# A fused sliding-window attention and expert-attention kernel: outputs of the last batch in two parts, one transfer for the last 64 rows, a new order list

## The chip, the cores and the metric

The kernel runs on one NeuronCore of one Trainium2 chip. The metric is the device time of one launch in microseconds, as the median of several runs. Inputs and outputs lie in device memory (DRAM); the core computes from its on-chip memory (SBUF) and accumulates matmuls in eight PSUM banks of 128 x 512 floats. Five engines work beside each other, each with its own instruction queue, in program order: TensorE (PE, matmuls; PEld are its weight loads), VectorE (DVE), ScalarE (ACT), GpSimd (POOL), and SyncE (SP), which here only issues transfers. Engines wait for each other through semaphores.

## What is computed

Eight batches of 576 positions. First an attention over a window of 32 positions on either side, with 8 heads of 64; its output, heads side by side, is `x` of the second part: four experts, each a causal attention over all 576 positions with a head size of 64 and an output projection to 512, of which each position adds up its best two by a gate.

```python
scores = q @ k.T / 8;  mask = abs(pos[:, None] - pos[None, :]) <= 32
attn = softmax(where(mask, scores, -1e9));  x = heads_side_by_side(attn @ v)      # [8, 576, 512]

logits = x @ w_gate;  topk = best 2 of 4;  w = softmax(logits of those 2)
for e in range(4):
    a = softmax(causal((x @ wq[e]) @ (x @ wk[e]).T / 8))
    ye = a @ (x @ wv[e]) @ wo[e]
    out += where(e in topk, w[e], 0) * ye                                          # [8, 576, 512] float32
```

## The kernel before

The whole program is written out by hand as a list of steps, `ORDER` (lines 27 to 89). The loop at the end (line 607) takes one step after the other and calls the function of that name, which emits its instructions. As every engine runs its own instructions in program order, the list sets, for each engine, what stands before what; between engines only data and buffers make anyone wait. A step reads `name` + digits + optional `:engine` + optional `@banks`: `sc601@62` is the score matmuls of batch 6, head group 0, second half of the columns, into banks 6, 7 and 2, 3; `ye52:v@7` copies an output of batch 5 from bank 7 on VectorE. The letters behind the colon are v, g and a for VectorE, GpSimd and ScalarE; a load with `e` is issued by SP, with `f` by ScalarE's queue.

The steps of one batch, in the order in which data goes:

- `lq`, `lk`, `lv`: loads of q, k and v. A load waits for the last matmul that stands ahead of it in the list. `tq`, `tk` transpose q and k on VectorE, two instructions each. `vc` makes a shifted copy of v.
- `sc`, `ex`, `mk`: window scores (80 matmuls for one half of one head group), their exponential on ScalarE, their mask as a product on GpSimd or VectorE.
- `av`, `un`: probabilities times v, and the division by the sum (VectorE). `xt`, `xf`, `xb`: transposition of the result on TensorE, its copy out of PSUM, its copy to bf16. A `zz` is four matmuls of zeros.
- `ga`, `gt`, `ge`, `gm`, `gu`: the gate: matmul, transposition and maximum, exponential, choice of two, weights. `gu` is four small VectorE instructions.
- `pp`, `pe`: q and k of two experts (pair `j`), and their copy out of PSUM; `pv`, `ve`: the same for v.
- `ps`, `xe`, `se`: causal scores, their exponential (ScalarE), their mask (GpSimd).
- `po`, `oe`: for pair `j` of experts, probabilities times v in five tiles of 128 positions and two experts, 30 matmuls; then on VectorE a reciprocal of the sums, its product with the gate's weight, and the product with the result, into `OE`.
- `dt`: a transposing transfer of `OE` into `OTT`, issued by SP. For batch 7 the turn is made on TensorE in its place (`pt`, five transposes into one bank, and `ot`, the copy into `OTT`).
- `py`, `ye`, `st`: the output projection from `OTT`, its copy into a buffer `Y`, the store. `w` is 0 or 1 for 256 positions each and 2 for the last 64. In batch 7, `w` 0 and 1 are split into single tiles of 128 (`py701` is batch 7, `w` 0, second tile).

There are three buffers `Y`, chosen by `YSB[(3 * b + w) % 3]`, so by `w` alone: a copy `ye` of batch b waits until the store of the same `w` of batch b - 1 has landed. For `w` = 2 the 64 positions lie as two halves of the 512 columns on 128 partitions, and line 597 stores each half by a transfer of its own.

Of the kernel before, what the change touches and what calls it, by code (L numbers as in the profile page):

```python
# [9 lines left out]
BF16 = mybir.dt.bfloat16  # L10
# [9 lines left out]
S = 576  # L20
# [7 lines left out]
    s_zero s_ones lk000:e lq000:e lv03 lk012:e tk000:e lq011:f zz1@0 zz0@0 lq012:e lk011:e s_ident s_mask lq100:e  # L28
    tq000:e sc000@02 lk100:e s_warm ex0001@2 tq011:e ex0000@0 sc001@46 ex0010@4 lv01 lv02 zz4@0 tk012:e tq012:e
    tk011:e sc010@02 mk0001:g mk0000:v ex0100@0 tq100:e lv00 tk100:e ex0101@2 zz2@4 lk110:e sc011@40 ex0011@6 zz3@2  # L30
    ex0110@4 mk0011:g vc00:a lv04 s_pads lq110:e lw00 sc101@26 vc01:a mk0101:v mk0100:v lw11 ex0111@0 av01@4 un01@4
    mk0110:g mk0010:g mk0111:g av00@0 un00@0 av04@4 lw2 xt00@0 un04@4 xf00:a@0 av03@4 ex1010@2 ex1011@6 tk110:e lw01
    av02@0 lq200:e un03@4 sc100@26 lk200:e xt02@4 ex1001@6 xf02:a@4 un02@0 xt01@0 xb02:a tq110:e mk1011:g sc110@64
    ex1000@2 xb00:g cw11:g xf01:v@0 lw10 tq200:e cw01:g mk1000:g cw2:g sc111@20 ex1101@4 xb01:a cw10:g lv13 lv11
    pp011@4 ex1100@6 lwg cw00:a tk200:e pp010@6 lv12 lv10 ex1110@2 pp000@2 pe011:a@4 pe000:v@2 pp001@4 ex1111@0
    sc201@02 lq210:e pe001:v@4 pe010:a@6 ps002@6 mk1010:v ga0@4 mk1111:v mk1110:v mk1100:v lv14 mk1101:g mk1001:g
    vc10:g ex2010@0 vc11:g lk210:e gt0@4 ps001@0 xe002@6 se002 ex2011@2 xe001@0 pv00@6 sc200@20 lq300:e tq210:e
    ve00:a@6 ex2000@2 av12@6 un12@6 ex2001@0 ps011@2 xe011@2 lq310:e ge0@4 av13@0 un13@0 ps000@2 pv01@5 xe000@2 av10@6
    tk210:e ps03@0 lv21 un10@6 xt11@2 ve01:a@5 xe03@0 av11@0 xf11:a@2 lk300:e un11@0 lv22 av14@5 ps010@2 un14@5 gm0@4
    xt10@6 xf10:v@6 xe010@2 xt12@5 xf12:a@5 sc211@02 lv20 lv24 tq300:e lv23 xb12:a ex2110@0 ga1@5 gt1@5 gu0@4 sc210@60  # L40
    ex2111@2 xb11:a mk2010:g mk2000:g se010 mk2011:g xb10:g lq400:e mk2001:g pp110@2 ex2100@6 ex2101@0 pp101@6 ge1@5
    tk300:e pp111@0 pe110:a@2 pe101:a@6 vc20:a mk2111:g mk2101:g se011 lw3 lk310:e pe111:v@0 gm1@5 gu1@5 tq310:e
    mk2100:g vc21:g pp100@2 pe100:a@2 pv11@4 sc300@60 mk2110:g ex3000@6 ex3001@0 pv10@2 ve10:a@2 av21@6 lq410:e av23@0
    un21@6 av22@2 un23@0 ps101@6 un22@2 lv32 ps100@0 av24@5 cw3:g se000 mk3000:g se001 xe100@0 xe101@6 se03 un24@5
    xt21@2 lv31 xt22@5 lk400:e xf22:v@5 xf21:a@2 ve11:v@4 xb22:g ps012@0 av20@6 sc301@24 un20@6 xt20@6 xe012@0
    ex3011@4 lv33 tk310:e ex3010@2 mk3001:g xb21:g se012 xf20:a@6 po00@0 lq500:e ps13@4 ps112@2 po01@6 xe112@2 oe00@0
    xe13@4 ps102@0 xe102@0 sc311@24 oe01@6 mk3011:g mk3010:g ex3111@4 lk500:e xb20:g sc310@60 pp201@4 ex3110@2 lv30
    lk410:e ex3100@6 ex3101@0 ps111@2 ps110@6 pp200@0 pe201:a@4 tk400:e xe111@2 lv34 pp211@4 tq400:e pp210@2 xe110@6
    lv42 pe210:a@2 pe200:v@0 pe211:v@4 tq410:e pv20@6 ve20:a@6 sc400@02 mk3101:g mk3111:g mk3100:g vc31:g se101
    mk3110:g dt00 se100 vc30:g tk410:e dt01 ex4000@0 ex4001@2 lv40 sc401@46 ps202@0 ga2@2 ex4011@6 mk4011:g se110 se13  # L50
    mk4001:g se102 lv43 pv21@3 av33@6 lq600:e xe202@0 av30@0 ve21:a@3 ex4010@4 gt2@2 py02@3 ge2@2 ye02:a@3 lk600:e
    av32@4 gm2@2 un33@6 un30@0 av34@3 py01@6 lv41 ye01:a@6 gu2@2 un32@4 un34@3 po10@0 xt32@2 lv50 xf32:a@2 av31@4
    ps23@6 xe23@6 oe10@0 ps211@2 un31@4 xe211@2 xt31@0 ps210@6 mk4000:g xe210@6 sc411@42 xf31:v@0 lv51 lq510:e xt30@0
    ex4110@4 ex4111@2 tk500:e tq500:e xf30:a@0 sc410@64 ex4101@4 py00@2 ye00:v@2 ex4100@6 se112 xb32:g mk4010:g se111
    xb31:g ps201@0 vc41:g ps200@4 xb30:g se202 vc40:g pp301@6 xe201@0 xe200@4 pp311@0 lk510:e pe301:v@6 sc501@24
    pe311:a@0 sc500@60 ex5010@2 tq510:e lv44 pp300@2 ex5011@4 lv53 ex5000@6 pp310@4 po11@6 ex5001@0 pe300:a@2 tk600:e
    pe310:a@4 oe11@6 ps300@0 ps301@2 mk4101:g mk4110:g mk4111:g av43@4 se200 mk4100:g lk610:e pv31@6 xe300@0 av40@0
    xe301@2 av41@2 un43@4 un40@0 ve31:a@6 lv54 av42@4 un41@2 ps212@6 dt10 ps302@0 xe212@6 ga3@2 xe302@0 av44@3 un42@4
    ps33@4 xe33@4 tq600:e dt11 un44@3 st00 xt41@6 xf41:a@6 lv61 lv52 xt40@0 gt3@2 ge3@2 gm3@2 xt42@3 xf40:a@0 xf42:a@3
    sc600@46 ex6001@6 ex6000@4 mk5000:g lq610:e tk510:e mk5010:g se201 se300 se210 se302 xb41:g se212 se23 se211  # L60
    xb42:a pv30@0 gu3@2 lv63 ve30:v@0 xb40:a sc510@64 mk5011:g ex5100@6 lv64 lq710:e pp401@2 pe401:a@2 pp411@0
    pe411:a@0 po20@6 oe20@6 st02 st01 ex5101@4 py10@2 ye10:a@2 st10 sc511@04 sc601@62 ex5111@4 lk710:e ex5110@0
    ex6011@2 po21@4 ps310@0 ex6010@6 tk610:e oe21@4 tq610:e se33 ps312@2 pp410@6 xe310@0 xe312@2 vc50:g mk6000:g
    mk5100:g mk5001:g vc51:g mk5101:g pe410:a@6 se301 pp400@0 pe400:a@0 po30@4 mk5111:g se310 lq700:e ps311@2 oe30@4
    xe311@2 ps400@6 av51@0 un51@0 mk5110:g av52@2 av50@4 lv60 lk700:e py12@0 dt21 xe400@6 un52@2 un50@4 ye12:a@0
    pv41@1 av53@6 ve41:a@1 ps401@2 ps412@4 tq700:e xe412@4 ga4@0 dt20 gt4@0 av54@1 st12 xe401@2 un54@1 ge4@0 se400
    se412 xt50@4 mk6010:g un53@6 gm4@0 pv40@2 xf50:a@4 xt52@1 se312 xb50:a mk6011:g ve40:a@2 xt51@6 mk6001:g gu4@0
# [10 lines left out]
    oe50@0 po41@4 xe602@6 oe41@4 ps610@0 av71@2 xe610@0 av70@6 un71@2 ps600@4 ps510@0 dt41 xe510@0 un70@6 av72@2
    xe600@4 av73@6 ps612@0 xe612@0 ps601@4 un72@2 av74@2 un73@6 st30 ga6@3 un74@2 ps63@6 ps512@0 xe601@4 gt6@3 xe63@6
    xt71@4 ge6@3 xe512@0 se510 se600 se612 se512 xt72@2 xf71:a@4 py31@6 gm6@3 gu6@3 se611 dt40 py40@0 xt70@4 xf72:a@2  # L80
    xb72:g ye40:a@0 xb71:g po51@2 ye31:v@6 py32@0 oe51@2 xf70:a@4 py42@1 pv71@4 pv61@5 st31 st40 py41@6 dt51 xb70:g
    se602 se63 pv60@2 ye41:a@6 ve60:v@2 se610 se601 ve71:v@4 pv70@6 ve61:a@5 dt50 po61@2 ve70:a@6 pp710@4 po60@6
    ye32:v@0 st32 oe61@2 st41 pp711@2 pe710:a@4 oe60@6 pe711:a@2 pp701@4 ye42:v@1 ps710@6 pe701:a@4 ps712@0 xe712@0
    py50@2 ye50:v@2 pp700@4 xe710@6 py51@0 pe700:a@4 ps73@6 ps711@2 xe73@6 st42 se73 se710 se712 xe711@2 ps701@4 dt60
# [563 lines left out]
```

## Time and profile before

| | us |
|---|---|
| median of 3 runs | 236.13 (235.8 to 241.28) |
| the profiled execution, as timed | 235.27 |
| its span in the profile | 233.5 |
| busy: PE, PEld | 213.4, 169.7 |
| busy: DVE, ACT, POOL | 180.2, 146.3, 148.9 |

The span is counted from the core's first instruction to its last. Busy time of PE is modelled and holds the pipeline's own delay, so a busy PE is not PE at its fastest. The page gives the engines' busy shares in forty slices, the transfers by queue, the chain of waits (from the last instruction back to what released each step), the groups of instructions by line, operation and shape, and the transfers by kind with the median time from issue to landing. A line of a group reads: line, engine, operation, output <- input, shape, count | busy us, mean ns of one | idle us of the engine just before them, and what ended that idle time. The trace answers the same for any stretch of the span, given in microseconds from its start. Lines of helpers stand for several steps: L177 is every matmul, L171 and L169 are all copies on VectorE or GpSimd and on ScalarE, L292 are `tq` and `tk`, L337 `ex`, L341 `mk`, L514 `xe`, L517 `se`, L552 to L554 `oe`, L567 `dt`, L598 to L603 `st`.

### The profile page before, as it was taken

How to read it: one execution, taken by the hardware profiler on the slowest of the kernel's cores; microseconds unless marked ns; L12 is line 12 of the kernel's file. 1: busy time of each engine (PE TensorE's matmuls, PEld its weight loads, DVE VectorE, ACT ScalarE, POOL GpSimd, SP SyncE). 2: the span in 40 equal slices, each digit the busy share in tenths (PEclk: the TensorE clock that was granted, in tenths of full speed). 3: DMA queues.
4: the chain of work that ended last, by engine and by line, in shares of the span. 5: the costliest groups of instructions: out<-in, count | busy, mean ns of one | idle time of the engine just before them, and what ended most of it. 6: DMA issues, size and time to landing. Idle time of an engine off the chain costs nothing.

```text
span 233.5 us, 12227 instructions
## 1 busy us (share of the span) xinstructions
PE 213.4 (91%) x5472; PEld 169.7 (73%) x5486; DVE 180.2 (77%) x354; ACT 146.3 (63%) x223; POOL 148.9 (64%) x180
## 2 busy tenths in 40 slices
PE   6497999989999999899999969999999999999970
PEld 1374877868798977786898758987788787786540
DVE  1998889999977996779889449998577477645671
ACT  2067356856756876368768558577686667746931
POOL 7028195754996876989957598398978662630500
PEclk9999999999999999999999999999999999999998
DMA  6988889867867789956669975696752016284865
GB/s 234 317 207 237 208 253 207 247 207 194 212 210 202 235 261 113 247 151 149 170 151 157 280 272 188 156 81 170 171 152 93 6 25 150 101 139 137 251 213 204
DMA packets 64549, 42.94 MB, mean 184 GB/s; under 512 B 54768, under 2 KB 55792, under 8 KB 64496
## 3 DMA queue, kind: packets, MB, share of 16 engines
q1 hardware_dynamic: 64352, 41.86, 70.0%
q8 instruction: 43, 0.70, 1.3%
q10 hardware_dynamic: 144, 0.29, 0.4%
q14 instruction: 10, 0.08, 0.1%
HBM read 30.42 MB, written 9.44 MB: 171 GB/s over the span
## 4 chain that ended last, share of the span: by engine, by line
PE 59%; DVE 19%; POOL 7%; DMA 7%; issue 5%; ACT 1%; DVEq 0%; POOLq 0%; ACTq 0%
PE PS L177 55%; DVE Tkn L292 6%; DVE Tqn L292 4%; PE PS L180 4%; DVE A L341 3%; DMA V<-in_v_dram 3%; POOL A L341 3%; POOL V L171 2%; DMA kn<-in_k_dram 2%; DVE XN L369 2%; DMA out_dram<-Y 2%; POOL XTB L171 1%; POOL ATE L517 1%; DVE XTF L171 1%; DVE RC L368 0%
## 5 line engine op out<-in xcount | busy, mean ns | idle before, releaser
L341 POOL TENSOR_TENSOR A<-A,MASKP 128x576 f32<-128x576 f32 x57 | 80.0, 1416 | 20.0 <-ACT A L337 19.6
L514 ACT ACTIVATE ATE<-PS 128x1024 bf16<-128x1024 f32 x48 | 47.3, 1024 | 16.5 <-PE PS L177 14.0
L337 ACT ACTIVATE A<-PS 128x576 f32<-128x576 f32 x64 | 38.9, 651 | 23.7 <-PE PS L177 22.7
L177 PE MATMUL PS<-Tqn,Tkn 32*64 32x128 f32 (+3 forms) x2560 | 46.4, 276 | 6.8 <-DVE Tqn L292 4.6
L177 PEld LDWEIGHTS PS<-Tqn,Tkn 32*64 32x64 f32 x2560 | 40.4, 135 | 15.2 <-DVE Tqn L292 6.3
L177 PE MATMUL PS<-V,A 128*64 128x65 f32 (+1 forms) x1280 | 40.8, 223 | 3.4 <-DVE XN L369 1.2
L177 PEld LDWEIGHTS PS<-V,A 128*64 128x64 f32 (+1 forms) x1280 | 36.9, 132 | 7.9 <-issue 3.0
L292 DVE STREAM_TRANSPOSE Tkn<-kn 128x576 f32<-128x576 f32 (+1 forms) x34 | 37.4, 1180 | 6.4 <-DMA kn<-in_k_dram 5.6
L517 POOL TENSOR_SCALAR_AFFINE_SELECT ATE<-ATE 128x256 bf16<-128x256 bf16 x64 | 25.6, 414 | 24.7 <-ACT ATE L514 20.7
L292 DVE STREAM_TRANSPOSE Tqn<-qn 128x576 f32<-128x576 f32 (+1 forms) x34 | 37.2, 1178 | 0.6 <-DMA qn<-in_q_dram 0.6
L171 POOL COPY V<-V 64x2048 f32<-64x2048 f32 (+1 forms) x12 | 21.0, 1748 | 6.3 <-DMA qn<-in_q_dram 2.8
L369 DVE TENSOR_TENSOR XN<-PS,RC 128x512 f32<-128x512 f32 x32 | 22.1, 692 | 1.2
L177 PE MATMUL PS<-WO,OTT 128*128 128x512 bf16 (+1 forms) x85 | 18.4, 342 | 1.5 <-DVE OTT L171 0.8
L180 PE MATMUL PS<-ident,XN 128*128 128x128 f32 x144 | 19.1, 278 | 0.0
L169 ACT COPY XTF<-PS 128x128 f32<-128x128 f32 (+1 forms) x23 | 13.6, 631 | 7.6 <-PE PS L180 6.9
L177 PE MATMUL PS<-XTB,WK 128*128 128x288 bf16 x128 | 17.9, 286 | 0.4 <-issue 0.3
L177 PE MATMUL PS<-WV,XTB 128*128 128x256 bf16 (+1 forms) x192 | 18.2, 256 | 0.0
L169 ACT COPY Y<-PS 128x1024 f32<-128x1024 f32 (+2 forms) x13 | 9.8, 752 | 13.2 <-PE PS L177 13.2
L177 PE MATMUL PS<-XTB,WQ 128*128 128x288 bf16 x128 | 17.9, 286 | 0.0
L169 ACT CAST QKE<-PS 128x576 bf16<-128x576 f32 x21 | 13.4, 645 | 6.8 <-PE PS L177 6.8
L177 PEld LDWEIGHTS <-ATE 128*128 128x128 bf16 x448 | 16.1, 97 | 2.0 <-issue 0.4
L171 DVE COPY Y<-PS 128x1024 f32<-128x1024 f32 (+2 forms) x13 | 11.6, 894 | 7.5 <-PE PS L177 4.4
(76 smaller groups left out, 273.0 us busy)
## 6 DMA issues: line engine op xcount, KB each, us to landing
kn<-in_k_dram SPq DMA_DIRECT2D x15, 576.0 KB, 4.8
qn<-in_q_dram SPq DMA_DIRECT2D x15, 576.0 KB, 5.1
V<-in_v_dram SPq DMA_DIRECT2D x32, 256.0 KB, 4.2
out_dram<-Y SPq DMA_DIRECT2D x14, 512.0 KB, 4.0
V<-in_v_dram SPq DMA_DIRECT2D x8, 128.0 KB, 4.6
out_dram<-Y SPq DMA_DIRECT2D x16, 64.0 KB, 2.9
out_dram<-Y SPq DMA_DIRECT2D x4, 256.0 KB, 2.6
kn<-in_k_dram SPq DMA_DIRECT2D x2, 288.0 KB, 5.7
```

Of the source, the lines that this page charges most:

```text
L169: nc.scalar.copy(o, i)
L171: eng(c).tensor_copy(o, i)
L177: last_pe[0] = nc.tensor.matmul(*a, **kw)
L180: last_pe[0] = nc.tensor.transpose(*a)
L292: nc.vector.transpose(T[:, :].rearrange("q (p o) -> q o p", o=18)[:, o0:o1], n_[:, o0:o1, 32 * dh:32 * dh + 32])
L337: nc.scalar.activation(AT[(2 * b + g) % NAT_][half][p], two(b0)[:, :, 0:HS], EXP, scale=scale_att)
L341: eng(c).tensor_tensor(out=ap, in0=ap, in1=MASK[:, None, HS * half:HS * half + HS].to_broadcast([128, 2, HS]), op=MULT)
L369: nc.vector.tensor_tensor(out=XN[T // 2][:, T % 2, :].rearrange("p (g h d) -> p g h d", g=2, h=4), in0=u[:, :, :, 0:64], in1=rc[:, :, :, N ...
L514: nc.scalar.activation(chunk(ATE[(2 * b + j) % len(ATE)], ch), two(b0), EXP, scale=scale_moe)
L517: nc.gpsimd.affine_select(ap, ap, pattern=[[0, n], [1, w]], compare_op=IS_GE, fill=0.0, base=0, channel_multiplier=-1)
```

## The change

Four functions are rewritten, so that `po`, `oe`, `pt` and `ot` may take a part of the five tiles: part 0 is tiles 0 and 1, part 1 is tiles 2 to 4. A step with a part uses one bank instead of two, with both experts of the pair side by side in it. Only batch 7 uses parts: `po71` becomes `po710` and `po711`, and so on. Then `st` changes in two ways: the last 64 rows go out as one transfer whose destination is written as 2 x 64 x 256, and a step that carries `:t` goes to ScalarE's queue.

```diff
+    TPARTS = [(0, 2), (2, 5)]
+
+    def half(at):
+        return (at[0], 0, NQT) if len(at) == 1 else (at[1], *TPARTS[at[0]])
+
+    def outs(at):
+        b0, t0, t1 = half(at)
+        n = t1 - t0
+        if len(at) == 1:
+            return two(b0)[:, :, 0:65 * n].rearrange("p e (t c) -> p e t c", c=65)
+        return one(b0)[:, 0:130 * n].rearrange("p (e t c) -> p e t c", e=2, c=65)
+
-    def po(c, b, j, b0):
+    def po(c, b, j, *at):
         A, V = ATE[(2 * b + j) % len(ATE)], VE[b % 2]
+        U = outs(at)
+        t0, t1 = half(at)[1:]
         for eo in range(2):
-            for qt in range(NQT):
-                o = PS[:, b0 + eo, 65 * qt:65 * qt + 65]
+            for qt in range(t0, t1):
+                o = U[:, eo, qt - t0, :]
...
-    def oe(c, b, j, b0):
-        p_ = two(b0)[:, :, 0:325].rearrange("p e (t c) -> p e t c", c=65)
-        rg, O = RG[j], OE[(2 * b + j) % NOE]
+    def oe(c, b, j, *at):
+        t0, t1 = half(at)[1:]
+        p_ = outs(at)
+        rg, O = RG[j][:, :, t0:t1], OE[(2 * b + j) % NOE]
...
-    def ot(c, b, j, b0):
-        copy(c, OTT[b % 2][:, j, 0:S], one(b0).bitcast(BF16)[:, 0:S])
+    def ot(c, b, j, *at):
+        b0, t0, t1 = half(at)
+        n = min(128 * t1, S) - 128 * t0
+        copy(c, OTT[b % 2][:, j, 128 * t0:128 * t0 + n], one(b0).bitcast(BF16)[:, 0:n])
...
     def st(c, b, w, *at):
         if w == 2:
-            for s in range(2):
-                nc.sync.dma_start(out[b, 512:576, 256 * s:256 * s + 256], ysb(b, w)[64 * s:64 * s + 64, 0, 0:256])
+            (nc.scalar if c == "t" else nc.sync).dma_start(out[b, 512:576, :].rearrange("r (s x) -> s r x", s=2),
+                                                           ysb(b, w)[:, 0, 0:256])
         elif at:
             r = 256 * w + 128 * at[0]
-            nc.sync.dma_start(out[b, r:r + 128, :], ysb(b, w)[:, at[0], :])
+            (nc.scalar if c == "t" else nc.sync).dma_start(out[b, r:r + 128, :], ysb(b, w)[:, at[0], :])
```

The list is new as a whole. It has the same steps, but for the parts of batch 7 (8 steps become 16); their order, banks and copying engines differ. No `st` in it carries `:t`, so every store stays on SP's queue; one load more, `lk011`, is on ScalarE's. Of the 64 `mk`, VectorE has 4 where it had 7; of the 26 `ye`, ScalarE has 17 where it had 13. The beginning and the end of both lists:

```diff
-    s_zero s_ones lk000:e lq000:e lv03 lk012:e tk000:e lq011:f zz1@0 zz0@0 lq012:e lk011:e s_ident s_mask lq100:e
-    tq000:e sc000@02 lk100:e s_warm ex0001@2 tq011:e ex0000@0 sc001@46 ex0010@4 lv01 lv02 zz4@0 tk012:e tq012:e
+    lq011:f lk012:e s_ones s_warm s_zero zz0@0 tq011:e lq012:e tk012:e tq012:e lk011:f s_ident lv03 lq000:e s_mask
+    lk000:e lv00 tk011:e sc011@02 lv02 lv01 ex0111@2 zz4@4 ex0110@0 sc010@24 lk100:e s_pads zz1@0 tq000:e tk000:e
...
-    ye51:v@0 xe701@4 ga7@6 gt7@6 ps702@0 xe702@0 se701 ps700@2 dt61 st50 se711 py52@7 ge7@6 xe700@2 ye52:v@7 py60@4
-    gm7@6 se702 po71@0 gu7@6 st51 py61@2 oe71@0 se700 po70@6 pt71@0 oe70@6 st52 ye60:a@4 ot71:v@0 st60 py62@1 pt70@4
-    ot70:v@4 ye61:a@2 st61 py701@0 py710@2 ye701:v@0 py700@3 ye62:a@1 st62 st701 py72@0 ye710:v@2 py711@1 ye700:a@3
-    st710 ye711:a@1 st700 st711 ye72:v@0 st72
+    dt61 py51@6 ve70:v@0 xe711@2 py50@4 ps710@0 se701 se702 ps712@2 ye51:a@6 ga7@6 dt60 ye50:v@4 xe710@0 py52@7
+    xe712@2 pv71@0 gt7@6 se700 se73 py61@4 st51 po700@1 ve71:a@0 ge7@6 po701@0 ye52:a@7 se712 ye61:a@4 py60@2 se711
+    se710 st50 st52 po711@7 gm7@6 gu7@6 oe700@1 oe701@0 py62@6 st61 ye60:a@2 pt701@0 po710@1 oe711@7 ot701:a@0 st60
+    pt711@7 ot711:v@7 ye62:a@6 pt700@0 ot700:a@0 py710@6 st62 py711@0 oe710@1 pt710@1 ye710:a@6 st710 ye711:a@0 st711
+    ot710:v@1 py700@2 ye700:a@2 st700 py701@3 py72@2 ye701:a@3 st701 ye72:v@2 st72
```

More of the change, by code (lines that the diff above doesn't have):

```diff
@@ L33 @@
[L33 to L67, printed above, removed]
@@ L78 @@
[L78 to L82, printed above, removed]
@@ new lines @@
+    xe03@0 ps001@2 xe001@2 tk200:e av11@6 sc200@02 un10@4 lw2 se012 mk1110:g mk1111:g ps011@4 ex2001@2 un11@6 av13@6
+    av12@2 xe011@4 lv22 lv20 ps002@4 lq300:e un13@6 un12@2 ex2000@0 xe002@4 ps000@0 xt10@6 xe000@0 sc201@24 cw2:g
+    ex2010@2 ga0@0 ex2011@4 xf10:a@6 tq210:e xt11@2 tk210:e lk300:e gt0@0 xf11:a@2 av14@1 sc210@46 un14@1 mk2010:g
+    mk2001:g se000 se002 se001 xb11:g se010 xb10:a ge0@0 gm0@0 ex2101@6 xt12@1 lv23 xf12:v@1 xb12:a ex2100@4 mk2100:g
+    tq300:e mk2101:g pv00@2 se011 lv21 lk310:e pp101@6 pe101:v@6 pp100@4 gu0@0 ve00:a@2 lk400:e pe100:a@4 pp110@2
@@ new lines @@
+    pe110:v@2 ps102@6 pv01@0 tk300:e pv11@1 sc211@42 lv24 lv33 ve11:a@1 xe102@6 ex2111@2 ex2110@4 ga1@1 gt1@1 ve01:v@0
+    lq310:e sc301@62 pp111@4 ex3011@2 pv10@2 ge1@1 gm1@1 lv30 lw3 gu1@1 vc21:g se03 mk2000:g tk310:e mk2111:g vc20:a
+    ex3010@6 po00@0 mk2011:g ve10:a@2 mk2110:g mk3011:g mk3010:g cw3:g se102 oe00@0 av23@6 pe111:a@4 un23@6 av22@2
+    un22@2 av20@4 lk410:e sc300@06 av21@2 lv34 ex3000@0 ps112@0 ex3001@6 xe112@0 ps101@6 un20@4 tq310:e lv31 xe101@6
+    un21@2 xt21@4 lq400:e lv41 av24@0 xf21:v@4 un24@0 ps100@2 xt20@6 xe100@2 po01@4 oe01@4 xt22@0 xf20:a@6 tk400:e
@@ new lines @@
+    pe600:a@4 py30@0 mk7000:g mk7100:g mk7001:g vc71:g st22 py31@6 se511 oe41@2 dt40 mk7101:g ye30:a@0 st30 ps510@2
+    ps612@4 ye31:a@6 av71@0 av70@6 xe510@2 un71@0 mk7110:g av73@2 py32@0 un73@2 pv61@1 xe612@4 ve61:a@1 av72@4 dt41
+    ps602@2 xe602@2 ye32:v@0 av74@0 ga6@1 un72@4 ps63@4 un70@6 un74@0 xe63@4 ps611@2 gt6@1 xe611@2 ps600@6 st32 py42@0
+    xt70@4 ye42:v@0 xe600@6 ge6@1 gm6@1 xf70:v@4 xt71@2 xf71:a@2 xt72@0 se612 se602 se611 xb70:g py40@6 xf72:v@0 se63
+    se510 se600 pv60@4 ps601@2 gu6@1 ye40:a@6 xb72:a xb71:a ps610@0 xe601@2 xe610@0 ve60:v@4 pp701@6 pe701:a@6 py41@4
```

67 lines of the change are left out of this document (46 added, 21 removed).

## The prediction

> **What bounds the kernel now.** I read the page first (share of each engine, forty slices), then the busy time by stretches, then the chain of waits and the queue of SP at the end, then the groups by shape, from which the terms below are priced.
>
> ```profile
> span 233.5 us, 12227 instructions
> ...
> PE   6497999989999999899999969999999999999970
> ```
>
> TensorE is full from the second tenth of the span to its last slice. What can move is what stands before, in the single dent at the 24th slice, and behind. The stretches, cut at list steps (8.7 is the first score matmul, 55.8 is `sc211`; columns: stretch, its length, busy us and instructions of PE, PEld, DVE, ACT, POOL, clock, DMA share, GB/s):
>
> ```profile
> 8.70:55.80 47.10, 43.39 (x1273) 34.35 (x1276) 44.37 (x81) 27.27 (x42) 24.18 (x21) 1.00 0.84 226
> 55.80:111.40 55.60, 54.30 (x1571) 44.46 (x1579) 47.56 (x90) 38.23 (x59) 48.05 (x52) 1.00 0.82 196
> ```
>
> Up to `sc211` it is VectorE that is short: 44.37 of 47.10 us busy, while TensorE has 47.10 - 43.39 = 3.7 us of holes and GpSimd stands idle 22.9 us. After it VectorE has room (47.56 of 55.60) and TensorE has 1.3 us of holes. The other places:
>
> ```profile
> 130.00:140.00 10.00, 7.72 (x241) 6.00 (x242) 3.85 (x7) 5.52 (x9) 7.72 (x6) 1.00 0.92 279
> 213.70:227.50 13.80, 12.02 (x163) 7.20 (x164) 9.09 (x24) 9.53 (x14) 3.47 (x9) 1.00 0.66 207
> ```
>
> 2.3 us are lost at 130 to 140, 1.8 us in the last batch's outputs, and from 227.5 to the end of the span, 6 us, TensorE has all but nothing to do. The waits of TensorE put 1.9 us of the first loss down to no semaphore at all:
>
> ```profile
> PE PS L177 <- issue: 3.1, 4, 1.9
> ```
>
> The end, by the chain of waits and by SP's own queue (start, us, what):
>
> ```profile
> 223.23 3.98 DMA out_dram<-Y
> ...
> 228.19 0.42 DVE Y L171
> ```
> ```profile
> 224.21 1.28 SPq L598 DMA_DIRECT2D out_dram<-Y  x2
> 226.89 2.60 SPq L601 DMA_DIRECT2D out_dram<-Y  x4
> 229.58 1.53 SPq L598 DMA_DIRECT2D out_dram<-Y  x2
> ```
>
> The Y buffers bind here: there is one for each w, and a copy into it waits until the store of the batch before has landed (3.98 us for `st60`). Behind the last copy, `ye72`, done at 228.61, come 0.97 us until SP has issued the row stores before it, two issues (1.53), the landing and the close: 233.5 - 228.61 = 4.9 us.
>
> **The change, part by part.** The sum is made against the profiled execution, 235.27 us (span 233.5), which lies 0.86 us under the median of the runs, 236.13.
>
> *Stores on ScalarE's queue.* `st` takes that queue where its step carries ":t". No step of the new list does, and the order of instructions has all stores on SP. Cost nothing, and this part of the change does not happen. The one transfer that does move there, `lk011`, waits for the four dummy matmuls of `zz0`; behind it stand ScalarE's table load and a warm-up, and the first exp needed neither for some microseconds: nothing.
>
> *The list, first quarter.* I compare what stands ahead of the same step, `sc211`, in both lists. On TensorE the new list has more ahead: `sc210`, `pp100`, `pp101`, `pp110`, and the short `ps012`, `ps102`, `pv11`. On VectorE it has `tq300` and `tk300` more (four transposes), two `pe`, the four small operations of `gu0`, four small `xf` pieces, and less: three `mk` and two whole `xf`.
>
> ```profile
> 58.63 1.39 PE L177 MATMUL PS<-Tqn,Tkn 32*64 32x96 f32 x80
> ...
> 209.19 0.86 PEld L177 LDWEIGHTS <-WQ 128*128 128x128 bf16 x8
> ```
> ```profile
> L292 DVE STREAM_TRANSPOSE Tkn<-kn 128x576 f32<-128x576 f32 x30 | 35.0, 1244 | 6.4 <-DMA kn<-in_k_dram 5.6 <-PE PS L177 0.8
> ...
> L341 DVE TENSOR_TENSOR A<-A,MASKP 128x576 f32<-128x576 f32 x7 | 8.9, 1310 | 0.0
> ...
> L171 DVE CAST QKE<-PS 128x576 bf16<-128x576 f32 x11 | 8.3, 756 | 3.9 <-PE PS L177 3.7
> ...
> L171 DVE COPY XTF<-PS 128x1024 f32<-128x1024 f32 x5 | 6.1, 1217 | 0.6 <-PE PS L180 0.5
> ...
> L448 DVE TENSOR_TENSOR G<-PS,su 128x20 f32<-128x20 f32 x8 | 1.6, 194 | 0.3
> ...
> L171 DVE COPY XTF<-PS 128x128 f32<-128x128 f32 x4 | 1.0, 284 | 0.6 <-PE PS L180 0.6
> ```
>
> VectorE: 4 x 1.244 + 2 x 0.756 + 4 x 0.194 + 4 x 0.284 - 3 x 1.310 - 2 x 1.217 = +2.0 us. TensorE: 1.39 + 3 x 0.86 + about 0.5 for the sixteen short matmuls (an estimate) = 4.5 us more work done. With VectorE as the bound in both, 4.5 - 2.0 = 2.5 us are won. Bounds: 0, if TensorE itself becomes the bound earlier, and 3.7, all its holes there. I take 2.5. The `mk` go to GpSimd, seven more ahead of `sc211`, with five more `se`:
>
> ```profile
> L341 POOL TENSOR_TENSOR A<-A,MASKP 128x576 f32<-128x576 f32 x57 | 80.0, 1416 | 20.0 <-ACT A L337 19.6
> ...
> L517 POOL TENSOR_SCALAR_AFFINE_SELECT ATE<-ATE 128x256 bf16<-128x256 bf16 x64 | 25.6, 414 | 24.7 <-ACT ATE L514 20.7
> ```
>
> 7 x 1.416 + 5 x 0.414 = 12 us into 22.9 idle: hidden, and 1 us or so if the order is awkward. ScalarE takes more copies where it is idle a third of the time: nothing. The middle of the list I cost at nothing, since TensorE's matmuls cover what moves there as long as each load keeps its lead; the stall at 130 to 140 has no named cause, so one like it may stay or go (-1.9 to 0): 0.
>
> *The last 64 rows as one transfer.* Today two issues, each of 64 rows, one behind the other. In the new program the destination is written 2 x 64 x 256, its outermost count 2. Every other transfer of this kernel counts 64 or 128 rows outermost. How such a transfer is dealt to the DMA engines no row of before shows, so I bound it from both sides. Below: over 16 engines, 8 packets each, and one issue (half of 1.53) is saved. Above: over two engines, 64 packets of 1 KB each. The price of a byte, from a stretch in which the engines are full:
>
> ```profile
> q1 hardware_dynamic: 791, 1.46, 99.4%
> ```
>
> That is 134 to 138: 0.994 x 16 x 4 us for 1.46 MB, 43.6 us for a MB on one engine, 2.9 us for 64 KB. Sixteen engines would need 0.36. So the two-engine case costs 2.5 us more for each store, and as much for whatever lies behind it on those two engines. I take two engines, because the outermost count is the only thing that sets this transfer apart, and weigh the other as a rival. The Trainium skill, "DMA: Bandwidth & Descriptors", section "Rules for kernel authors", says the same against this change: an outermost dimension below 16 confines a transfer to at most that many engines. No run here shows it yet; by it the sum is the two-engine one.
>
> Who waits for it: the next batch's copy into the same Y buffer. At the end three stores stand in one chain: `st52`, `ye62`, `st62`, `ye72`, `st72`.
>
> ```profile
> DMA to landing us min/median/max: 2.0/2.7/4.1
> ```
> ```profile
> 219.45 0.42 DVE L171 COPY Y<-PS 128x256 f32<-128x256 f32 x1
> ```
> ```profile
> L169 ACT COPY Y<-PS 128x256 f32<-128x256 f32 x4 | 1.5, 376 | 4.0 <-PE PS L177 4.0
> ...
> L169 ACT COPY Y<-PS 128x512 f32<-128x512 f32 x2 | 1.2, 586 | 3.2 <-PE PS L177 3.2
> ```
>
> `ye52` ends today at 219.87, and the matmuls left behind `py52` are the same in both lists but for `pv71`. In the new list it runs on ScalarE behind an exp and `ve71`, so at about 220.5 on the same scale. Then: store 2.7 + 2.5 = 5.2, `ye62` 0.4, store 5.2, `ye72` 0.4, and the last store to the end: 4.9 less SP's 0.97 and one issue (0.77), plus 2.5 = 5.7. Sum 220.5 + 16.9 = 237.4 against 233.5: +3.9 us. Between, in batch 3, `st32` is followed in the list by `py42` after some 3.5 us of matmuls; `ye42` stands on VectorE and waits for it, up to 2 us, and behind it VectorE has the copies for batch 7 and TensorE the bank of `xt72`. I take +1.5 (0 to 2).
>
> *Outputs of the last batch in two parts.* `po`, `oe`, `pt`, `ot` of batch 7 for tiles 0 and 1 and for 2 to 4. It adds two `oe` (three short instructions each) and two `ot`, and lets the first part's transpose start while the second is multiplied. Today it is 6.9 us from the end of `gu7`, 221.74, to the end of `ye72`:
>
> ```profile
> 221.55 0.19 DVE L448 TENSOR_TENSOR G<-PS,su 128x20 f32<-128x20 f32 x1
> ```
>
> In pieces I come to about 6.0, an estimate from the groups, with the four row copies one after the other on ScalarE (586 ns each). That is 0.9, with the issue saved (0.77) and half of SP's 0.97 some 2.1 us, but only where the stores don't bind. In the two-engine case the chain above is longer, and this is hidden whole.
>
> Sum: 235.27 - 2.5 + 1.5 + 3.9 = 238.2.
>
> **The rivals.** *Faster: dealt over 16 engines.* Then the store chain is shorter than the matmuls, and 235.27 - 2.5 - 2.1 = 230.7 us. For it: the stores of 64 rows land in the shortest time of all but one kind,
>
> ```profile
> out_dram<-Y SPq DMA_DIRECT2D x16, 64.0 KB, 2.9
> ```
>
> and nothing in the page says that a transfer may use fewer engines. Against: no row shows an outermost count of 2.
>
> *Slower: the two engines hold up what is behind.* The other five merged stores stand ahead of loads and of the OTT transposes on the same queue. Where a load has less than 2.5 us between landing and use, TensorE waits for the rest. For it: the DMA share is 0.82 to 0.92 for most of the span. Against: most loads are issued ten and more microseconds of matmuls ahead. Two of the five in full: 238.2 + 2 x 2.5 = 243.2. It decides from the point where such a load or transpose is in flight behind the store.
>
> **How the numbers follow.** Chances: forecast 0.45, sixteen engines 0.27, slower rival 0.28. The forecast's own range, with the early gain from 0 to 3.7 and `st32` from 0 to 2, is 235 to 241. The range that holds eight in ten reaches to both rivals: 230.5 to 243.5. A measurement of this kernel tells about 2% from no change, that is 231.4 and 240.9. Faster: 0.20 of the sixteen-engine case and 0.03 of the forecast, 0.23. Slower: 0.25 of the rival and 0.08 of the forecast, 0.33. Within: 0.44.
>
> **What would show it.** `sc211` should start some 2 us later than today's 55.8, with 4.5 us more matmul work behind it. The merged stores should take about 5 us to land where the 64-row ones took 2.9; if they take under 3, the sixteen-engine rival holds. `ye62` and `ye72` should wait for DMA out_dram<-Y, and the last store's landing end the span some 6 us behind `ye72`. If loads or the transposes show up as releasers of TensorE or VectorE between 60 and 200 us, it is the slower rival. It is wrong altogether if the middle of the list brings a new stall of several microseconds that no store has to do with.

## The result, and the profile after

The changed kernel takes 245.08 us (median of 4 runs, 244.18 to 248.43) where the kernel before, run beside it on the same chip, takes 237.84 (235.8 to 241.28): ratio 1.0374, 95% interval 1.0315 to 1.0432. It is 3.7% slower. The forecast was 238.2 with a range up to 243.5; the result lies outside. The profiled execution took 245.29 us, with a span of 243.5. Runs in a second, slower state are left out of every ratio given here, so that a ratio is not always the quotient of the two medians; the profiles of e10, e12 and f4 are of such runs.

The page of the changed kernel: busy time, the forty slices of TensorE and of its granted clock, and the stores by kind (count, KB each, median us from issue to landing):

```profile
span 243.5 us, 12244 instructions
...
PE   3597699999999999999999999999999998959740
...
PEclk9999799999999999999999999999999999997985
...
out_dram<-Y SPq DMA_DIRECT2D x8, 128.0 KB
out_dram<-Y SPq DMA_DIRECT2D x4, 256.0 KB, 4.7
```

The dent at the 24th slice is gone. Dips have come in the 5th slice (6) and in the 36th (5), the 38th and 39th are emptier, and the clock row falls below 9 in the 5th and 37th, where the kernel before has it full. The eight merged stores have no landing time on the page, and the four row stores of batch 7, which did not change, take 4.7 us where they took 2.6. Their line in the kernel before:

```profile
out_dram<-Y SPq DMA_DIRECT2D x4, 256.0 KB, 2.6
```

The missing median has a reason in the trace. There a store of the kernel before ends with 16 updates of its semaphore, and the core has 16 DMA engines. The updates of the stores, counted in the trace:

```
kernel        transfer                      updates   issue to landing, us, last three
before        64 rows x 1 KB, 16 of them    16        2.8, 2.8, 2.5 (batches 6, 7, 7)
changed       2 x 64 x 1 KB, 8 of them       3        4.8, 5.6, 4.8 (batches 5, 6, 7)
both          256 rows or 128 rows          16
```

Of the three, one comes 0.9 to 1.2 us behind the issue and two at the landing, which I read as two engines. The packets in the trace say the same: the 128 packets of the last merged store are under way for 3.3 us, two at a time for 2.8 of them; those of the last two 64-row stores of the kernel before for 1.3 us, up to 17 at a time. The waits of the changed kernel (engine, line, what it waited for: us in total, times, the longest):

```profile
DVE Y L171 <- DMA out_dram<-Y: 5.9, 2, 4.6
...
ACT Y L169 <- DMA out_dram<-Y: 2.8, 4, 1.1
PE PS L177 <- DMA OTT<-OE: 2.8, 1, 2.8
```

The end of its chain of waits (start, us, what):

```profile
213.03 6.40 DMA OTT<-OE
219.43 0.05 issue
219.47 5.32 PE PS L177 x57
...
225.57 0.38 ACT Y L169
225.95 0.02 issue
225.97 4.82 DMA out_dram<-Y
...
230.87 0.37 ACT Y L169
231.24 0.03 ACT OTT L169
231.27 5.63 DMA out_dram<-Y
...
237.37 0.42 DVE Y L171
```

Read from the bottom: the last copy, `ye72`, stood until the store `st62` had landed (5.63 us); `ye62` before it stood until `st52` had landed (4.82 us); and `ye52`, at 225.57, came late because TensorE had waited for a transpose, `dt51`, which took 6.40 us. What `dt51` stood behind is in SP's own queue (start, us, what):

```profile
212.23 0.69 SPq L616 DMA_DIRECT2D out_dram<-Y  x1
213.03 4.52 SPq L586 DMA_TRANSPOSE OTT<-OE  x3
```

L616 is the merged store `st42`, issued 0.8 us ahead of it; it lands at 217.3, `dt51` at 219.4.

### The profile page after: what moved, and what is told of

Its sections match the earlier page's. It is cut to its first block, busy times and chain, and to the rows that moved or that the text cites. A ratio compares the mean times of both kernels' runs of the same rounds, so it can differ in the third digit from the quotient of the medians.

```text
span 243.5 us, 12244 instructions
## 1 busy us (share of the span) xinstructions
PE 216.0 (89%) x5486; PEld 170.3 (70%) x5486; DVE 170.7 (70%) x359; ACT 156.2 (64%) x228; POOL 145.5 (60%) x178
## 4 chain that ended last, share of the span: by engine, by line
PE 71%; DMA 12%; DVE 7%; ACT 4%; issue 3%; DVEq 0%; ACTq 0%
PE PS L177 65%; DMA out_dram<-Y 6%; PE PS L180 6%; DMA OTT<-OE 3%; DVE Tqn L292 2%; DMA qn<-in_q_dram 2%; DVE XN L369 1%; ACT V L169 1%; DVE Tkn L292 1%; DMA V<-in_v_dram 1%; ACT XTF L169 1%; DVE XTF L171 1%; DVE RC L368 0%; ACT XTB L169 0%; DVE Y L171 0%
## 5 line engine op out<-in xcount | busy, mean ns | idle before, releaser
L341 POOL TENSOR_TENSOR A<-A,MASKP 128x576 f32<-128x576 f32 x60 | 84.2, 1426 | 24.1 <-ACT A L337 23.9
L517 POOL TENSOR_SCALAR_AFFINE_SELECT ATE<-ATE 128x256 bf16<-128x256 bf16 x64 | 24.7, 406 | 30.9 <-ACT ATE L514 30.7
L177 PE MATMUL PS<-WO,OTT 128*128 128x512 bf16 (+1 forms) x96 | 20.9, 362 | 4.4 <-DMA OTT<-OE 2.8
L180 PE MATMUL PS<-ident,XN 128*128 128x128 f32 x144 | 20.4, 284 | 0.3 <-DVE XN L374 0.2
L177 PE MATMUL PS<-XTB,WK 128*128 128x288 bf16 x128 | 18.5, 286 | 0.2
L180 PEld LDWEIGHTS PS<-ident,XN 128*128 128x128 f32 x144 | 16.1, 144 | 3.6 <-issue 0.9
L169 ACT COPY XTF<-PS 128x1024 f32<-128x1024 f32 (+1 forms) x19 | 14.5, 783 | 6.1 <-PE PS L180 5.8
L171 POOL CAST XTB<-XTF 128x128 bf16<-128x128 f32 (+1 forms) x16 | 10.3, 663 | 13.5 <-ACT XTF L169 7.2
L169 ACT COPY Y<-PS 128x1024 f32<-128x1024 f32 (+2 forms) x17 | 13.2, 800 | 8.0 <-PE PS L177 5.2
L171 POOL COPY V<-V 64x2048 f32<-64x2048 f32 (+1 forms) x10 | 16.7, 1679 | 2.3 <-DMA V<-in_v_dram 1.2
```

The lines of the kernel that those rows point to most:

```text
L169: nc.scalar.copy(o, i)
L171: eng(c).tensor_copy(o, i)
L177: last_pe[0] = nc.tensor.matmul(*a, **kw)
L180: last_pe[0] = nc.tensor.transpose(*a)
L341: eng(c).tensor_tensor(out=ap, in0=ap, in1=MASK[:, None, HS * half:HS * half + HS].to_broadcast([128, 2, HS]), op=MULT)
L517: nc.gpsimd.affine_select(ap, ap, pattern=[[0, n], [1, w]], compare_op=IS_GE, fill=0.0, base=0, channel_multiplier=-1)
```

## The experiments

Where the time is now late can be estimated by laying both kernels side by side at equal matmul work done. As the lists differ in order, the lag in the first 100 us depends by several us on how a matmul is weighed: at 58 us the changed kernel is 1 to 5 us behind. Later the estimates agree: it is level to about 1.5 us between 140 and 200 us, 1.4 behind at 215, 5.5 behind at 226 (the stretch with `py51`), 6.7 behind at its last matmul, and it ends 3.3 us later still. So there were three suspects: the merged stores, the parts, the list.

Each kernel of the table is the changed kernel, the kernel before, or one of the experiments with an edit more, and all of them compute the whole. The ratio is to the kernel before on the same chip.

| kernel | what | median, us | ratio (95%) |
|---|---|---|---|
| changed | | 245.08 | 1.0374 (1.0315 to 1.0432) |
| e1_two_stores | changed, two stores of 64 rows | 240.1 | 1.0124 (1.0041 to 1.0207) |
| e2_merge_only | before, merged store | 242.54 | 1.0209 (1.0110 to 1.0307) |
| e3_parts_only | before, batch 7 in parts | 237.03 | 0.9989 (0.9952 to 1.0026) |
| e4_two_b567 | changed, two stores in batches 5 to 7 | 242.34 | 1.0224 (1.0095 to 1.0353) |
| e5_two_b4 | changed, two stores in batch 4 | 244.83 | 1.0392 (1.0323 to 1.0461) |
| e6_two_b0123 | changed, two stores in batches 0 to 3 | 245.98 | 1.0410 (1.0333 to 1.0488) |
| e7_rows64 | changed, one store, 64 rows outermost | 239.02 | 1.0133 (1.0064 to 1.0202) |
| e10_last_y | changed, last outputs not in Y | 248.37 | 1.0301 (1.0212 to 1.0389) |
| f3_before_rows64 | before, one store, 64 rows outermost | 237.64 | 1.0020 (0.9971 to 1.0069) |
| e9_head | e7, two loads issued earlier | 237.97 | 1.0083 (1.0037 to 1.0129) |
| f1_zz | e9, dummy matmuls as before | 240.51 | 1.0168 (1.0089 to 1.0246) |
| f2_zz_pads | f1, pads cleared later | 238.09 | 1.0104 (1.0041 to 1.0167) |
| e11_dt51 | e7, `dt51` earlier | 241.67 | 1.0184 (1.0118 to 1.0250) |
| f4_t_stores | e7, two stores on ScalarE's queue | 238.46 | 1.0073 (1.0013 to 1.0132) |
| e12_best | before, parts, last outputs not in Y | 236.16 | 0.9977 (0.9943 to 1.0011) |

**The parts of the change, one by one.** First the store put back to two transfers, in the changed kernel:

```diff
-            (nc.scalar if c == "t" else nc.sync).dma_start(out[b, 512:576, :].rearrange("r (s x) -> s r x", s=2),
-                                                          ysb(b, w)[:, 0, 0:256])
+            for s in range(2):
+                nc.sync.dma_start(out[b, 512:576, 256 * s:256 * s + 256], ysb(b, w)[64 * s:64 * s + 64, 0, 0:256])
```

> The changed kernel with only the last 64 rows undone: two stores of 64 rows again, in every batch; list and parts as changed. Theory M (the merged store lands late, and Y copies and OTT transposes wait for it): the waits of VectorE at 196 us, of TensorE at 213 us and the chain of stores behind 226 us go, together 8 to 10 of the span's 243.5 us, so about 235 to 237 us as timed. Theory L (the new list is bad by itself): it stays above 242. A share each, as the early stretch of the changed kernel is 2.6 us late at the same matmul work: 238 to 240.

It measured 1.0124: of the 3.7% some 2.5 are the merged store, and 1.2 stay, each to about one per cent by the intervals. The wait of TensorE for OTT falls but does not go; the waits of this kernel:

```profile
PE PS L177 <- DMA OTT<-OE: 1.3, 1, 1.3
```

Then the merge alone, in the kernel before:

```diff
-            for s in range(2):
-                nc.sync.dma_start(out[b, 512:576, 256 * s:256 * s + 256], ysb(b, w)[64 * s:64 * s + 64, 0, 0:256])
+            nc.sync.dma_start(out[b, 512:576, :].rearrange("r (s x) -> s r x", s=2), ysb(b, w)[:, 0, 0:256])
```

> The kernel before with only the merged store of the last 64 rows; the old list, no parts. Theory M: in the old list two such stores stand in one chain with ye62 and ye72 at the end as well, each 2 to 3 us later, and dt transposes stand behind some: 4 to 8 us slower than before, so 240 to 245. Theory L: within 1 us of before, or faster by half a microsecond for the issue saved.

1.0209, that is some 5 us, with the old list. Its chain of waits ends in the same stair as that of the changed kernel:

```profile
223.76 6.14 DMA out_dram<-Y
...
230.00 0.38 ACT Y L169
230.38 0.02 issue
230.39 4.79 DMA out_dram<-Y
...
235.31 0.42 DVE Y L171
```

Then the parts alone, in the old list, the steps of batch 7 written in by hand:

```diff
-    gm7@6 se702 po71@0 gu7@6 st51 py61@2 oe71@0 se700 po70@6 pt71@0 oe70@6 st52 ye60:a@4 ot71:v@0 st60 py62@1 pt70@4
...
+    gm7@6 se702 po710@0 po711@1 gu7@6 st51 py61@2 oe710@0 oe711@1 se700 po700@6 po701@7 pt710@0
+    oe700@6 pt711@1 oe701@7 st52 ye60:a@4 ot710:v@0 ot711:a@1 st60 py62@1 pt700@4 pt701@5 ot700:v@4 ye61:a@2
+    ot701:v@5 st61 py701@0 py710@2 ye701:v@0 py700@3 ye62:a@1 st62 st701 py72@0 ye710:v@2 py711@1 ye700:a@3
```

> The kernel before with only batch 7's outputs in two parts: the old list up to gu7, then the parts by hand; two stores of 64 rows. The prediction put the parts at about 0.9 us gained where no store binds: 0 to 1.5 us faster than before. If the parts cost (more small VectorE and ScalarE steps in a row), 0 to 1.5 us slower.

No difference can be measured. The merged store and the list are what costs.

**Which of the merged stores.** The changed kernel with two transfers in some batches, one in the others:

```diff
+            if b in (5, 6, 7):
+                for s in range(2):
+                    nc.sync.dma_start(out[b, 512:576, 256 * s:256 * s + 256], ysb(b, w)[64 * s:64 * s + 64, 0, 0:256])
+            else:
...
```

> The changed kernel with two stores of 64 rows in batches 5, 6 and 7 alone, merged in 0 to 4. Theory M: the chain st52, ye62, st62, ye72, st72 goes back to matmul pace, 4 to 5 us faster than the changed kernel (about 240 to 241), while TensorE's wait before py51 at 216 us, behind st42, stays at about 3 us. If the end is not set by these stores: no change, 245.

> The changed kernel with the 64-row store in two transfers in batch 4 alone. Queue theory (the transpose dt51 stands behind st42's one transfer on the same engines, and py51 waits for it): the wait of TensorE for OTT before py51 falls from 2.8 us to about 1.3, as where all stores are in two, and the half clock that followed it goes; 1.5 to 3.5 us faster than 245.1, that is 241.6 to 243.6. Rival (py51's wait is the list's, not the store's): the wait stays, 245.

> The changed kernel with the 64-row store in two transfers in batches 0 to 3 alone. If only the last four merged stores cost anything, what goes is ye42's wait for st32 (some 1 us or less, hidden behind the later waits or not): 244 to 245.1. If the merged stores also hold up the loads behind them in the middle of the span, 1 us or more for each: 242.5 or less.

Two transfers in the last three batches bring 1.0374 down to 1.0224, with intervals that overlap. Those of batches 0 to 3 bring nothing that can be measured. They land earlier there too, 1.9 to 4.0 us from issue to landing in e6 where the merged ones of the changed kernel took 4.7 to 6.2; but of the copies into the same buffer only `ye42` waits for one of them. Batch 4 is the odd one. In the profile the store does what was expected; the waits of e5:

```profile
DVE Y L171 <- DMA out_dram<-Y: 5.5, 2, 4.3
...
PE PS L177 <- DMA OTT<-OE: 1.4, 1, 1.4
```

TensorE's wait falls from 2.8 to 1.4 us, the stair at the end stays, and the stretch of matmul work around `py51` shrinks from 10.1 us to 7.2 (the kernel before: 6.0). Yet the time does not move: 1.0392. At the same matmul, e5's profiled execution was already 2.2 us behind the changed kernel's at 87 us, in part through stalls of TensorE that no semaphore explains (3.1 us of them against 2.0 up to 88 us; below). Runs differ by this much, so a gain of a microsecond or two from batch 4 alone is neither shown nor excluded by the time.

**Merging, or the outermost count?** One transfer again, with the rows outermost:

```diff
-            for j in range(2):
-                for s in range(2):
-                    mm(PS[64 * s:64 * s + 64, at[0], 0:256], T[:, j, 512:576], WO[:, j, 256 * s:256 * s + 256],
-                       start=(j == 0), stop=(j == 1), skip_group_check=True)
+            for j in range(2):
+                mm(PS[0:64, at[0], :], T[:, j, 512:576], WO[:, j, :], start=(j == 0), stop=(j == 1))
...
-            copy(c, ysb(b, w)[:, 0, 0:256], one(at[0])[:, 0:256])
+            copy(c, ysb(b, w)[0:64, 0, :], one(at[0])[0:64, :])
...
+            (nc.scalar if c == "t" else nc.sync).dma_start(out[b, 512:576, :], ysb(b, w)[0:64, 0, :])
```

> The changed kernel with the last 64 rows still in one transfer of 128 KB, but written with the 64 rows outermost: the product goes to 64 partitions of 512 columns and is stored from there. If the outermost count of 2 is the cause, the store lands in 2 to 3 us, no wait for DMA out_dram is left in the last chain, and the time is that of two stores, 240.1, plus at most 1.5 us because the eight products use half of the array at a time: 239.5 to 241.6. If it is the merging itself (one transfer in place of two), the landings stay at 5 us and the time at 245.

This is the decisive run: the same 128 KB to the same place in one transfer, 1.0133, as with two transfers. The edit changes the product, the copy and the packets (2 KB) as well; but the two transfers of the kernel before have packets of 1 KB, as the merged store has, and 16 updates each. Its page:

```profile
span 237.9 us, 12197 instructions
...
out_dram<-Y SPq DMA_DIRECT2D x8, 128.0 KB, 3.0
out_dram<-Y SPq DMA_DIRECT2D x4, 256.0 KB, 2.6
```

The landing has a median again (3.0 us, with 16 updates each), and the row stores behind are back at 2.6 us. The transpose `dt51`, issued 0.7 us behind the store here too, lands in 2.8 us instead of 6.4. The same in the old list, with the same edit:

> The kernel before, its own list, with the last 64 rows as one transfer of 64 rows outermost. If one transfer costs nothing where its outermost count is 64, the same time or a little less, by an issue of SP at the end (0.8 us): ratio 0.994 to 1.002. If the merging itself costs, or the eight products on half of the array do, 1.005 or more; with the outermost count of 2 it was 1.0209.

1.0020 (0.9971 to 1.0069): one transfer has no cost and no gain that can be measured where its outermost count is 64; with a count of 2 it was 1.0209.

**The buffer or the engines?** In the end the stair could be paid through the copies that wait for a Y buffer, or through the two engines themselves. A kernel with four buffers `Y` in place of three answers nothing: its output is wrong, for a reason that is not known, and a copy in it still waits 5.8 us for a store (ratio 1.0550). In the changed kernel the last batch's outputs go to tiles that are free by then:

```diff
+        if b == B - 1:
+            return XN[w] if w < 2 else XN2[:, None, :]
         return YSB[(3 * b + w) % len(YSB)]
```

> The changed kernel, merged stores as they are, but the last batch's outputs are copied into the XN tiles, which are free by then, in place of Y: ye700 to ye72 wait for no store any more. What the end costs through the wait of ye72 for st62 (4.6 us in the profile) goes; what it costs through the two engines stays: st62 and st72 are worked off one behind the other, st72 landing some 3 us behind st62, at about 240 on the scale of the changed kernel in place of 242.6. So 241.5 to 243.5. If the wait for the buffer is not what sets the end, no change: 245. If the engines are no limit, 8 us less behind the last matmul is too much, but 239 or less would say so.

By the ratio, 1.0301, it is 243.2 us on a kernel before of 236.14, within what was expected, but its interval overlaps that of the changed kernel. Of its profile only lengths at the end are read, here SP's queue:

```profile
235.62 0.53 SPq L618 DMA_DIRECT2D out_dram<-Y  x1
236.89 3.37 SPq L622 DMA_DIRECT2D out_dram<-XN  x4
240.35 0.56 SPq L618 DMA_DIRECT2D out_dram<-XN  x1
```

The last store no longer waits for the one before to land: it is issued 4.7 us behind it instead of 6.6. But it then takes 6.5 us to land, 5.9 behind the other where 3 were expected, and from the last matmul to the end of the span it is 9.1 us where it was 9.0. The wait became a longer landing: in this one profile a free buffer wins nothing at the end. That it never would is not shown.

**What is left: the list.** With the store mended the changed list is still 0.7 to 1.8% slower, in seven kernels. Edits of e7 were tried on the places where the profile showed a loss. The loads that stood behind the first dummy matmuls, at the head of the list:

```diff
-    lq011:f lk012:e s_ones s_warm s_zero zz0@0 tq011:e lq012:e tk012:e tq012:e lk011:f s_ident lv03 lq000:e s_mask
+    lq011:f lk012:e lq012:e lk011:f s_ones s_warm s_zero zz0@0 tq011:e tk012:e tq012:e s_ident lv03 lq000:e s_mask
```

> As e7_rows64 (the 64 rows outermost, measured 239.0), with the loads lq012 and lk011 put ahead of the dummy matmuls zz0 in the list, so that they are issued at once and not when those have run (3.4 us). Theory: part of what is left over the kernel before (3 us) is lost at the head, where the first scores wait for these loads, and VectorE, short until 57 us, starts late by as much: the first score matmul 1 to 2 us earlier than 8.9, sc211 earlier by as much, 237 to 238.3. Rival: VectorE's order, with the clearing of pads ahead of two transposes, and not the loads, sets the first quarter: the first scores earlier, sc211 where it was, 239.

A miss in the profile: the first score matmul starts at 9.0 us, `sc211` at 64.6, no earlier than in e7 (8.7 and 64.3), because VectorE's transposes stand one behind the other from 4.9 us on, when `lq011` has landed. The ratio, 1.0083, overlaps that of e7. Then the dummy matmuls. The timeline of TensorE in e9 (start, us, what):

```profile
8.96 2.52 PE L177 MATMUL PS<-Tqn,Tkn 32*64 32x64 f32 x80 [5.59 <-DVE Tkn L292]
11.81 1.49 PE L177 MATMUL PS<-ZERO 128*128 128x512 bf16 x3 [0.33 <-issue]
13.23 2.22 PE L177 MATMUL PS<-Tqn,Tkn 32*64 32x96 f32 x80
15.39 1.04 PE L177 MATMUL PS<-ZERO 128*128 128x512 bf16 x3
```

Four blocks of them stand between the scores; the kernel before has two blocks ahead of the first score and three between. In f1 `zz1` goes back beside `zz0`, and in f2 the pads are cleared later as well (shown is f2; f1 leaves `s_pads` where it was):

```diff
-    ... s_zero zz0@0 tq011:e ... lk100:e s_pads zz1@0 tq000:e ... un01@6 un00@0 sc100@24
+    ... s_zero zz0@0 zz1@0 tq011:e ... lk100:e tq000:e ... un01@6 un00@0 s_pads sc100@24
```

> As e9_head, with the dummy matmuls zz1 put beside zz0, ahead of the first scores, where the kernel before has two such blocks and the changed list one. Between the scores a block takes 1.04 us of TensorE, which the scores behind it wait for. Theory: the list's cost at the head is in part this moved block: every step from the third score step on 1.0 us earlier, 0.4% less than e9 (ratio 1.0083): 1.003 to 1.005. Rival: the lists' difference comes from the stall and half clock near 25 us alone, and TensorE waits there longer: no change.

> As f1_zz, with the clearing of pads (2 us on VectorE) moved from ahead of the transposes tq000 and tk000 to behind the second un, near where the kernel before has it. If VectorE sets the first scores, up to 2 us earlier: ratio 0.995 to 1.0. If TensorE, which is full from 9 to 19 us, sets them, no change against f1.

Both are misses: 1.0168 and 1.0104. In the profiles they are 0.8 and 1.3 us ahead of e9 at `sc211`, as the theory had it for the block, but at `py51` 0.2 behind it and 0.7 ahead: what the head wins is in part or wholly lost again on the way. Last, the order of SP's queue around `dt51`, and the queue that the new code allows:

```diff
-    ps702@6 st41 oe51@4 st40 ps701@4 po60@2 oe60@2 xe700@0 dt50 st42 pv70@0 xe701@4 ps73@4 xe702@6 xe73@4 ps711@2 dt51
+    ps702@6 st41 oe51@4 dt51 st40 ps701@4 po60@2 oe60@2 xe700@0 dt50 st42 pv70@0 xe701@4 ps73@4 xe702@6 xe73@4 ps711@2
```

> As e7_rows64, with the transpose dt51 issued behind oe51, ahead of st40, dt50 and st42, in place of behind them. In e7 TensorE waited 1.2 us for Y ahead of py51 and the outputs behind it; in e1 it was 1.3 us for OTT. If the list's place for dt51 costs what is lost there, up to 1 us less: 238 to 239. If the copies of Y or VectorE's order set that place, no change: 239.

> As e7_rows64 (ratio 1.0133), with two of the last batch's row stores, st711 and st701, on ScalarE's queue, which the new code allows and the new list does not use. If SP's issues one behind the other cost at the end, up to 0.8 us less: ratio 1.010 to 1.013. If ScalarE's copies stand behind its issues, up to 1 us more.

`dt51` ahead of `st40` holds that store and `dt50` up instead: TensorE then waited 3.2 us for OTT, and the ratio is 1.0184. The stores on ScalarE's queue, 1.0073, cannot be told from e7.

**A version that beats both.** The parts could bring something only if the last batch's copies did not wait for Y, so both were put into the old list, with the second of the two last stores on ScalarE's queue:

> The kernel before with its own list, the parts of batch 7 written in by hand as in e3_parts_only, the last batch's outputs copied into the free XN tiles in place of Y, and the second of the two last stores on ScalarE's queue. In e3 the parts gave nothing because the copies into Y wait for the stores of batch 6. With that wait gone the gain that was worked out for the parts should show, up to 2.1 us: ratio 0.991 to 0.997, 234 to 236. If the end is bound by SP's issues or by TensorE and VectorE, no change: 0.999.

0.9977 (0.9943 to 1.0011): no gain that can be measured. No kernel here beats the kernel before.

## Why the prediction was wrong

**Two engines: right.** The forecast priced a merged store at 5.2 us; the last three took 4.8, 5.6 and 4.8. The rule it weighed, of the Trainium skill's "DMA: Bandwidth & Descriptors", section "Rules for kernel authors", is borne out by the three updates for each such store, by its packets and by e7: an outermost count of 2 costs, one of 64 doesn't. The sixteen-engine rival is dead.

**The chain of stores at the end: right.** From the end of `ye52` to the end of the span the forecast had 16.9 us; it is 243.5 - 225.95 = 17.5. In e10's profile, with a free buffer, it is as long.

**`ye42` behind `st32`: right in place and about in size, wrong in cause.** It waits 5.9 - 4.6 = 1.3 us, forecast 1.5. But in e1, with two transfers, it still waits 1.1 us: most of it comes from where the list puts store and copy, and little from the merging. e6, in which the wait for the store is gone, shows no gain.

**`:t` and the parts: right.** No store left SP's queue. The parts bring nothing that can be measured in e3 and e12, although 0.9 us, the forecast for stores that do not bind, would still lie within both intervals.

**The step that failed first: the early list, -2.5 us.** It rested on "With VectorE as the bound in both, 4.5 - 2.0 = 2.5 us are won". VectorE is not the bound in the new list. The stretch of the changed kernel from the first score to `sc211`, with the columns of the prediction's stretches:

```profile
8.70:63.70 55.00, 50.74 (x1400) 39.68 (x1401) 43.61 (x87) 33.33 (x46) 32.87 (x33) 0.97 0.81 219
```

VectorE is busy 43.61 us against 44.37 in the old list's stretch (the forecast had 2.0 more), and has 11.4 us of holes where it had 2.7. TensorE is busy 7.4 us longer, 50.74 of 55.00, and waits for VectorE less than 1 us of it: it has become the bound itself, the case for which the prediction had put the gain at 0. Of the 7.4 us, 4.5 are the added work that the forecast counted. The rest is about what two things take that it did not count: one dummy block more, 1.0 to 1.5 us in e9's timeline, and a stretch at half clock, 1.4 (e1, at full clock there, is busy 49.30 us). So `sc211` comes 7.9 us later, at 63.7 and not at 57.8. Adding up the bound engine's work said what the list needs; it did not say when each piece could start. At 200 us the changed kernel is about level with the kernel before and at 215 it is 1.4 us behind (2.3 in e1), where the forecast had won 2.5 and lost 1.5: 2.4 us of the 7.1 by which the profiled time missed.

**The step that failed second: `dt51` behind `st42` at nothing.** "The middle of the list I cost at nothing", and the transpose behind a merged store stood only in the slower rival, as "in flight behind the store". That is where it happened, in one place: the stretch with `py51` takes 10.1 us against 6.0, of which e1 and e5, with 7.3 and 7.2, put 2.8 on the store and 1.3 on the list. Only half of the 2.8 is the longer wait. The other half is the clock behind it, which no term of the prediction has: in the changed kernel the granted clock is 0.50 from 218.7 to 222.1 us. In e4, which has `st42` in one transfer too and waits as long, it stays at 1.00 and the stretch takes 8.7 us. The seven matmuls behind the wait, in the changed kernel:

```profile
219.47 2.97 PE L177 MATMUL PS<-WO,OTT 128*128 128x512 bf16 x7 [2.75 <-DMA OTT<-OE]
```

and in e4:

```profile
220.58 1.68 PE L177 MATMUL PS<-WO,OTT 128*128 128x512 bf16 x7 [2.67 <-DMA OTT<-OE]
```

These 4.1 us, the 2.4 above and 0.6 in the end chain are the 7.1. The rival had its mechanism right, but not its reach: loads in the middle were not held up (e6). That its number, 243.2, came near is in part luck, as 2.4 us of the miss are the list's.

**What stays open: the last 1%.** Of the list's own cost the runs show places, not a cause. The block of dummy matmuls, the pads, the two loads and the place of `dt51` were each changed, and none brought the time back. Left over are the stalls below: the new list has two of 1 us and more in most profiles, the old list one of 2 us in each and some smaller ones.

## What to carry to other kernels

Before two transfers are written as one, look at the outermost count of the new access pattern: 2 in place of 64 sent 128 KB through two engines, and what stood behind it on the queue, a transpose and four row stores, paid too. If the rows can be outermost, one transfer costs no more than two, as far as could be measured here (and won nothing). Where a new order is judged by the sum of a bound engine's work, ask of each engine's idle time in the new order as well: here VectorE's work did not grow by the 2 us of the sum (43.61 us against 44.37), and still the gain wasn't there. And a wait can cost more than its length: behind one of 2.8 us TensorE ran at half clock for 3.4.

## What the hardware showed besides

TensorE stalls without a semaphore, mostly at the same places of its instruction stream. Instructions arrive as 16 KB blocks; the page's row of the changed kernel gives 43 of them:

```profile
q8 instruction: 43, 0.70, 1.2%
```

In all twelve profiles with the new list there is a gap of 1.0 to 2.4 us in front of the 479th or 480th weight load, at 25 to 27 us; in ten of them, not in the changed kernel's and e6's, another of 1.3 to 2.7 us in front of the 2264th, at 91 to 94 us. The five with the old list have one of 2.1 to 2.7 us in front of the 3541st, at 135 to 138 us, which is the unnamed stall of the prediction; four of them have a smaller one, 0.8 to 1.3 us, in front of the 2392nd, and e2 has one of 1.9 in front of its 480th. Long or short, each of these gaps ends 1.2 to 1.6 us behind the end of the transfer of such a block. The timeline of e7:

```profile
27.60 2.29 PE L177 MATMUL PS<-Tqn,Tkn 32*64 32x64 f32 x86 [2.21 <-issue]
```

The Trainium skill, "Runtime: NRT & Kernel Launch", section "Instruction fetch mechanics", has the same block size and calls the cost of crossing a block mostly hidden; if these gaps are such crossings, some here are not. The times tie the gaps to the blocks closely, but no experiment moved a block.

After such a gap the clock can fall to half for 3.4 us. The changed kernel, with the columns as above:

```profile
27.60:31.00 3.40, 3.40 (x92) 3.12 (x92) 2.73 (x3) 1.84 (x3) 1.97 (x2) 0.50 0.20 45
```

TensorE is busy throughout, at a granted clock of 0.50. The gap ahead of it was 2.2 us. The Trainium skill, "TensorE: Matmul & The Clock Gate", section "What's actually happening", lets the clock fall after an idle window of about 3.4 us; the length of the slow stretch agrees, the gap was shorter. In e1, where the same gap was 1.0 us, the clock stayed full; in e5, after one of 2.1 us, it did too, so the length alone does not decide.
